# An FFT-and-experts kernel: the first batch's first stage is emptied without its scale, turned in fp32 by TensorE and split afterwards, with a new set of order constants

## The chip, the cores and the metric

The kernel runs on one core of one Trainium2 chip. The metric is the device time of one execution in microseconds (us); the medians are over three executions. TensorE is called PE here, VectorE DVE, ScalarE ACT, GpSimd POOL and SyncE SP, as the profile does.

## What is computed

Two parts follow each other. The first is a frequency-domain mixing layer, the second a top-1 mixture of experts on its output:

```python
X = np.fft.rfft(x, axis=1)                 # x: 8 batches x 2496 x 256
Yr = Xr @ w_r - Xi @ w_i + b_r
Yi = Xr @ w_i + Xi @ w_r + b_i
Y = soft_threshold(Yr, 0.01) + 1j * soft_threshold(Yi, 0.01)
y = np.fft.irfft(Y, n=2496, axis=1)        # 19968 tokens x 256

logits = y @ w_gate                        # 8 experts
e = argmax(logits); gate = softmax(logits)[e]
eom = sigmoid(y @ w_output_gate)[e]
out = gate * eom * (relu(y @ w1[e]) @ w2[e])   # 256 -> 1024 -> 256
```

## The kernel before

The transform of length 2496 = 39 x 64 is done in two stages of matrix products. For each of the 8 batches:

- **Stage 1** (`stage1_pair`, 11 pairs a batch): x as fp32 is the stationary operand, the 39-point table `f1t` the moving one. The result of a pair fills a PSUM bank. ACT and DVE empty it into the tile `at`, as a high and a low half in fp16 (L730, L731). Both are multiplied by the batch's scale `sx`, a power of two that `scales` works out from the squares and maxima of the whole batch (L444, L591, L628 to L630, a maximum over partitions through PE at L479, then L461 to L466).
- **The turn** (`load_a`): `at` has to be transposed, 10 pieces `p` of two planes each, into the ring of tiles `A`. Pieces named in `PT` are turned by PE, four fp16 products with the identity for each plane (L764), and emptied by ACT or DVE (L768, L769); the others by a transposing DMA of SP's queue (L750).
- **Stage 2** (L799, table `ct`), emptied into `xt` by ACT, DVE and one negation (L810, L811, L813 or L814); **the mixing** (L823 with the bias, L829 with the weights `whl`, 25 products for each of 10 steps), soft threshold into `z` and `zhl` (L844 to L849); **stage 3** (L859, table `gt`) into `bt`; a transposing DMA into `bdt` (L899); **stage 4** (L925), written to DRAM as `yd`.
- The gate's logits (L970, L980), and each token's rank in its expert. When four batches are through, and again when all eight are, the `routing` passes build lists of tokens by products of one-hot tiles (`ol`, `ob`; L1361, L1362, L1383, L1391 on PE). `indices` and `factors` end a pass (L1235, L1236).

The experts' part works on 160 tiles of 128 tokens. The tokens of a tile are gathered by an indirect DMA of POOL (L1491), scaled and split by DVE and ACT (L444, L1543, L1544), and transposed by DMA into `eT`. For two tiles of one expert, `up` makes four banks of 12 products each (L1651), emptied into `hh` by ACT (L1661) and then DVE (L1662). `down` makes 24 products for each tile in two halves of 12 (L1612). The first half reads what came from the first two banks of `up`, the second what came from the other two. A tile's result goes through ACT (L1628) and an indirect DMA of POOL (L1631) to the output. 18 tiles are shared by two experts ("mixed", with weights in `latebt` and `latebdt`).

While x of the first batch lands, `warm` puts products of a constant tile (L605) on PE wherever the plan has a gap before its time `WARM`.

The order of all this is not written out. Every operation asks for an engine with a due time, and the class `Issue` plays the engines forward with a duration for each operation: a free engine takes the ready operation with the earliest due time. The result is a fixed order of instructions for each engine; on the chip an engine works through its list and waits at semaphores. Due times are built from some sixty constants (`P`, `TP`, `TE`, `SA`, `UP`, `DN` and so on), so a change of them changes the order and nothing else. A name `bs` or `b` below is the mixing bias, `mx` the scale's partial sums, `yms` and `ymd` a tile's maxima.

Of the kernel before, what the change touches and what calls it, by code (L numbers as in the profile page):

```python
# [14 lines left out]
F32 = mybir.dt.float32  # L15
# [118 lines left out]
ET = mybir.EngineType  # L134
ORDERED = {ET.PE, ET.Activation, ET.DVE, ET.Pool, ET.SP}

P = 69.09
TP, TE, QT = -17.42, -31.89, 23.82
PT = (0, 1, 2, 3, 6, 8), (0, 1, 3, 6)
DK = 2.8  # L140
T1 = 0.91
S2 = 21.69
E1 = 55.44
DS = 3.78
ES = 11.46
Z1 = 52.83
Z2 = 35.62
IV = 0.04
IS = 2.69
GO = -30.77  # L150
R0 = 32.01
R1, G1 = -16.38, 0.17
GA = 0.7
W0 = 5.47
W1 = 30.1
TG = 33.24
HEAD = 15.0
LAG = dict(P=0.17, A=0.16, D=0.14, G=0.09, S=0.0)

RATE = 225e3  # L160
TAIL = 1.7
XL, TA, TB, YS, WL, WS = -73.83, -22.34, -36.29, 66.21, 6.06, 105.43

EARLY = dict(yg=3, yhl=2, eT=1, hh=1, o=1)
PLACES = dict(yg=6, yhl=5, eT=3, hh=2, o=5)
UP, DN = 1.08, 10.48
AHEAD = 6
FLUSH = {*range(T_A, T_ALL - 20, 16), *range(T_ALL - 20, T_ALL - 8, 4)}
# [3 lines left out]
LR = 10.75
QN, QY, QV, QX, QZ, QU = -2.96, 6.37, 247.7, 109.12, 39.86, 94.12
RA, QE = -34.21, -24.82
SA = 23.55
SE = 86.03
Z3 = -31.18
BE = 53.36
YE = 61.11
PB = -5.56, 0.44, 0.72, 8.7, 1.32, -0.16, 7.74, 6.51  # L180
XC = 7.0, 0.1, 5.4, 0.1, 3.0, 0.1
GL = 0.6
RT = -58.7
WT = 0.0
WF = -7.7
QO = -74.27
CB = 4
WARM = 40.0
OL = 2, 3
# [144 lines left out]
def tile_fft_moe(ctx, tc, x, w_r, w_i, b_r, b_i, w_gate, w_og, w1, w2, f1, f4, cmat, gmat, m16, out, dbg=None):  # L334
# [375 lines left out]
    def stage1_pair(b, g, r):  # L710
        xs = xt[b, g // 2]
        j0 = 2 * (g % 2)

        def f(i):
            pt = bank(i)
            pv = pt[:, :480].rearrange("p (k c w) -> p c k w", c=2, w=12)
            for j in range(2):
                for dh in range(2):
                    k, m = (P3, 6) if g < 10 else (2 * N1, 4)
                    fw = f1t[:k].rearrange("p (k c) -> p k c", c=6)[:, :, :m]  # L720
                    T.matmul(pv[:, dh, :, m * j:m * j + m], xs[:k, j0 + j, 128 * dh:128 * dh + 128], fw, start=True, stop=True)  # L721
            return pt[:, :480].rearrange("p (k c w) -> p k c w", c=2, w=12)

        i, pv = yield "P", r, T1, f, True
        used(b, g // 2)
        yield "sx", b
        sx = st[b, "sx"]
        m = 12 if g < 10 else 8
        hi, lo = (at[:, :, :, v, 12 * g:12 * g + m] for v in range(2))
        yield "A", r - SA, 0.66, lambda: A.activation(hi, pv[:, :, :, :m], AF.Copy, scale=sx)  # L730
        yield "D", r - SA, 0.68, lambda: V.scalar_tensor_tensor(lo, pv[:, :, :, :m], sx, hi, ALU.mult, ALU.subtract)  # L731
        io.free(i)
        give("s1")
        st[b, "n1"] += 1
        if st[b, "n1"] == 11:
            io.set("s1", b)

    def load_a(b, r):

        yield "s1", b  # L740
        if b == 0:
            yield "whl"
        for p in range(NP):
            yield slots["A"]
            a = st[b, "A", p] = ring(pm, [128, KP, 2, 2, 128], F16, "A", AN)
# [12 lines left out]

# [58 lines left out]
    def mix(b, p, r, xt_):  # L817
# [906 lines left out]
```

## Time and profile before

| | us |
|---|---|
| median of 3 executions (1417.12 to 1421.66) | 1419.6 |
| the profiled execution | 1415.86 |
| its span, first to last instruction | 1414.0 |
| PE busy | 1388.8 |
| DVE busy | 958.4 |
| ACT busy | 733.4 |
| POOL busy | 641.9 |

The span is what the trace covers; 1.9 us lie around it. A matmul's busy time is its latency, and neighbours overlap: 24 products of 256 columns that follow each other take 2.62 us in the chain of waits, 0.109 us each, though each shows 0.27 us of busy time. So a busy PE says that there was always a product under way, and the work itself is counted by the distance from one product to the next.

### The profile page before, as it was taken

Reading aid. Unit: us, or ns where it says so; the run is one execution under the profiler, and the core shown is the slowest. Engines: PE = TensorE matmul, PEld = TensorE weight load, DVE = VectorE, ACT = ScalarE, POOL = GpSimd, SP = SyncE. Lnnn points to the kernel's source line nnn. Section 1 sums busy time; section 2 is a strip of 40 time slices with the busy share of each in tenths; the row PEclk is TensorE's granted clock in tenths of the full one; section 3 lists DMA queues with packets and bytes.
Section 4 is the critical chain, followed back from the end, with each engine's and each line's share of the span. In section 5 each row is a group of like instructions: output and inputs, shape, how many; then the busy total and the mean of one; then the engine's idle time right before and its main releaser. Section 6 shows DMA issues by size and latency. Waiting matters only on the chain.

```text
span 1414.0 us, 40457 instructions
## 1 busy us (share of the span) xinstructions
PE 1388.8 (98%) x15696; PEld 1234.6 (87%) x15696; DVE 958.4 (68%) x2591; ACT 733.4 (52%) x1389; POOL 641.9 (45%) x718
## 2 busy tenths in 40 slices
PE   7999999999999999999999999999999999999998
PEld 5998888888888888888888888899999899899997
DVE  5787888789999887688899855454454455445441
ACT  4877777778786855444333344343343334334342
POOL 3464654446567655235554443334433433433322
PEclk9999999999999999999999999999999999999999
DMA  8699999998989696889562274556643566457541
GB/s 202 175 182 232 206 220 209 238 195 225 227 206 224 172 210 164 211 177 233 160 165 69 68 195 83 132 124 147 139 120 83 142 159 160 114 136 156 138 116 34
DMA packets 285994, 231.51 MB, mean 164 GB/s; under 512 B 239246, under 2 KB 248080, under 8 KB 279167
## 3 DMA queue, kind: packets, MB, share of 16 engines
q1 hardware_dynamic: 270377, 187.02, 56.0%
q0 software_dynamic: 15424, 41.90, 13.0%
q8 instruction: 123, 2.02, 0.6%
q14 instruction: 70, 0.57, 0.1%
HBM read 286.72 MB, written 58.52 MB: 244 GB/s over the span
## 4 chain that ended last, share of the span: by engine, by line
PE 80%; DVE 7%; issue 4%; DMA 3%; POOL 3%; SPq 1%; ACT 1%; POOLq 0%; ACTq 0%; DVEq 0%
PE ps L1651 26%; PE ps L1612 26%; PE ps L829 11%; PE ps L721 4%; PE ps L925 3%; PE ps L799 3%; PE ps L859 3%; POOL out L1631 1%; DMA x<-in_x 1%; PE ps L970 1%; DMA bdt<-bt 1%; PE ps L823 1%; PE ps L764 1%; PE ps L605 1%; DVE bt L875 1%
## 5 line engine op out<-in xcount | busy, mean ns | idle before, releaser
L1612 PE MATMUL ps<-wbuf,hh 128*128 128x256 f16 x3408 | 389.8, 273 | 0.0
L1651 PE MATMUL ps<-eT,wbuf 128*128 128x256 f16 x3408 | 387.5, 273 | 0.0
L1662 DVE SCALAR_TENSOR_TENSOR hh<-ps,hh 128x512 f16<-128x512 f32 x284 | 196.0, 691 | 254.3 <-ACT hh L1661 253.5
L1612 PEld LDWEIGHTS <-hh 128*128 128x128 f16 x3408 | 328.9, 98 | 42.0 <-issue 3.8
L1651 PEld LDWEIGHTS <-wbuf 128*128 128x128 f16 x3408 | 330.1, 98 | 40.2
L1631 POOL DMA_INDIRECT out<-o,sidx x160 | 165.2, 1033 | 361.7 <-ACT o L1628 334.7
L1661 ACT ACTIVATE hh<-ps 128x512 f16<-128x512 f32 x284 | 169.5, 597 | 237.0 <-PE ps L1651 235.1
L1491 POOL DMA_INDIRECT yg<-yd,gidx x160 | 163.1, 1020 | 137.5 <-DVE yhl L1544 81.1
L829 PE MATMUL ps<-whl,xt 128*128 128x256 f16 x1920 | 222.6, 273 | 0.0
L829 PEld LDWEIGHTS <-xt 128*128 128x128 f16 x1920 | 187.5, 98 | 31.6 <-issue 1.2
L1628 ACT ACTIVATE o<-ps,facd 128x256 f32<-128x256 f32 x142 | 67.0, 472 | 141.5 <-PE ps L1612 100.8
L1543 ACT ACTIVATE yhl<-yg,yss 128x256 f16<-128x256 f32 x142 | 68.2, 502 | 69.1 <-DVE yssi L455 53.6
L721 PE MATMUL ps<-f1t,x 117*128 117x120 f32 (+1 forms) x704 | 88.5, 280 | 8.3 <-DMA x<-in_x 8.0
L721 PEld LDWEIGHTS ps<-f1t,x 117*128 117x128 f32 (+1 forms) x704 | 84.6, 195 | 11.6 <-issue 9.6
L849 POOL TENSOR_TENSOR zhl<-z,zhl 128x512 f16<-128x512 f32 x63 | 75.3, 1196 | 28.4 <-ACT zhl L847 25.3
L848 POOL CAST zhl<-z 128x512 f16<-128x512 f32 x47 | 30.1, 641 | 109.5 <-DVE z L845 78.1
L1544 DVE SCALAR_TENSOR_TENSOR yhl<-yg,yss,yhl 128x256 f16<-128x256 f32 x142 | 66.8, 487 | 8.8 <-ACT yhl L1543 6.9
L844 ACT ACTIVATE zhl<-ps,sc 128x512 f32<-128x512 f32 x80 | 54.7, 686 | 32.6 <-PE ps L829 28.4
L1662 DVE SCALAR_TENSOR_TENSOR lategt<-ps,lategt 128x512 f16<-128x512 f32 x36 | 24.8, 688 | 68.8 <-ACT lategt L1661 68.8
L845 DVE SCALAR_TENSOR_TENSOR z<-ps,zhl 128x512 f32<-128x512 f32 x80 | 54.7, 685 | 20.0 <-ACT zhl L844 18.5
L1128 POOL TENSOR_TENSOR wsp<-wr,wsp 128x512 f16<-128x512 f32 x54 | 66.1, 1224 | 4.5
L925 PE MATMUL ps<-bdt,f4t 120*117 120x512 f16 x264 | 67.7, 379 | 0.0
(245 smaller groups left out, 2100.5 us busy)
## 6 DMA issues: line engine op xcount, KB each, us to landing
wbuf<-wd SPq DMA_DIRECT2D x142, 1024.0 KB
latebt<-wd SPq DMA_DIRECT2D x36, 1024.0 KB
latebdt<-wd SPq DMA_DIRECT2D x36, 1024.0 KB
yd<-yt SPq DMA_DIRECT2D x120, 158.4 KB
x<-in_x SPq DMA_DIRECT2D x106, 156.0 KB
wr<-in_moe_w SPq DMA_DIRECT2D x32, 512.0 KB
wd<-wsp SPq DMA_DIRECT2D x64, 256.0 KB
yg<-yd,gidx POOLq DMA_INDIRECT x160, 3.4
```

The source lines that it names most:

```text
L721: T.matmul(pv[:, dh, :, m * j:m * j + m], xs[:k, j0 + j, 128 * dh:128 * dh + 128], fw, start=True, stop=True)
L829: T.matmul(yp[:, 256 * j:256 * j + 256], xt_[:, v, 2 * dh + j, 64 - 64 * u:192 - 64 * u], whl[:, dh, vw, 256 * u:256 * u + 256], start=Fal ...
L849: yield either("G", r - Z3, 1.2, "D", r - Z3 + QY, 1.0, lambda e: e.tensor_tensor(zhl[:, 1], z, zhl[:, 0], ALU.subtract))
L925: T.matmul(pt[:P3], w, src[:, :, :, vb_], start=(n == 0), stop=(n == 2))
L1491: yield "G", r + 5.6 * POS[t] - 30, 1.0, lambda: G.indirect_dma_start(out=yg, out_offset=None, in_=src, in_offset=bass.IndirectOffsetOnAxi ...
L1543: yield "A", r - 10, 0.5, lambda: A.activation(yhl[:, 0], yg[:, :256], AF.Copy, scale=s)
L1612: T.matmul(st["pt", t][1][c * q:c * q + c, :256], hh[:, v, fc, 128 * n + c * q:128 * n + c * q + c], wq[:, fc // 2, vw, fc % 2], start=(fc ...
L1628: yield "A", r - DN, 0.47, lambda: A.activation(o, pt[:, :256], AF.Copy, scale=fac)
L1631: yield "G", r - DN, 1.0, lambda: G.indirect_dma_start(out=outs[POS[t] % 8], out_offset=bass.IndirectOffsetOnAxis(ap=sidx[:, t:t + 1], axi ...
L1651: T.matmul(pt[:, 128 * m * j:128 * m * (j + 1)][:, 64 * q:128 * m - 64 * (len(w) - 1 - q)], wq[:, dh, g // 4, vw, 128 * (g % 4):128 * (g % ...
L1661: yield "A", r, 0.6, lambda: A.activation(hv[:, 0], pt, AF.Relu)
L1662: yield "D", r, 0.69, lambda: V.scalar_tensor_tensor(hv[:, 1], pt, 0.0, hv[:, 0], ALU.max, ALU.subtract)
```

## The change

Three things. For batch 0, stage 1 is emptied by one operation, an unscaled copy in fp32 into the same memory as `at` (seen as fp32 through `at32`). It no longer waits for `sx`. The turn of batch 0 is done by PE alone, in fp32 (`turn_0`): four transposing products for a piece `p`, all in one bank; then ACT and DVE scale and split it into `A`. For this an fp32 identity is made by POOL once, in memory of `bdt`. The wait for the mixing weights `whl` moves from the start of the turn to the mixing. Last, all the constants of the order have new values.

```diff
-P = 69.09
-TP, TE, QT = -17.42, -31.89, 23.82
+P = 69.0665505
+TP, TE, QT = -40.317835, -48.0018785, 46.5639872
...
-UP, DN = 1.08, 10.48
+UP, DN = 3.5154488, -2.4275374
...
     at = pm.tile([128, K1, 2, 2, 128], F16, name="at")
+    at32 = at.rearrange("p k c v n -> p k c (v n)").bitcast(F32)
+    eye32 = bdt.rearrange("p a n -> p (a n)")[:, :256].bitcast(F32)
+    G.tensor_copy(eye32, t16[:, M16 - 256:M16 - 128])
...
         i, pv = yield "P", r, T1, f, True
         used(b, g // 2)
+        m = 12 if g < 10 else 8
+        if b == 0:
+            raw = at32[:, :, :, 12 * g:12 * g + m]
+            yield [("A", r - SA, 0.62, lambda: A.activation(raw, pv[:, :, :, :m], AF.Copy)),
+                   ("D", r - SA, 0.68, lambda: V.tensor_copy(raw, pv[:, :, :, :m]))]
+            io.free(i)
+            give("s1")
+            st[b, "n1"] += 1
+            if st[b, "n1"] == 11:
+                io.set("s1", b)
+            return
         yield "sx", b
...
     def load_a(b, r):
 
         yield "s1", b
-        if b == 0:
-            yield "whl"
         for p in range(NP):
             yield slots["A"]
             a = st[b, "A", p] = ring(pm, [128, KP, 2, 2, 128], F16, "A", AN)
+            if b == 0:
+                io.go(turn_0(p, a, r + 2 * DK * p + TP))
+                continue
...
+    def turn_0(p, a, r):
+
+        def f(i):
+            pt = bank(i)
+            for k in range(KP):
+                for dh in range(2):
+                    m = 256 * k + 128 * dh
+                    T.transpose(pt[:, m:m + 128], at32[:, KP * p + k, dh], eye32)
+            return pt.rearrange("p (m n) -> p m n", n=128)
+
+        i, pt = yield "P", r, 0.46, f, True
+        yield "sx", 0
+        sx = st[0, "sx"]
+        hi, lo = (a.rearrange("p k c v n -> p (k c) v n")[:, :, v] for v in range(2))
+        yield "A", r - TE, 0.6, lambda: A.activation(hi, pt, AF.Copy, scale=sx)
+        yield "D", r - TE, 0.68, lambda: V.scalar_tensor_tensor(lo, pt, sx, hi, ALU.mult, ALU.subtract)
+        io.free(i)
+        st["ta", 0] = st.get(("ta", 0), 0) + KP
+        io.set("ap", 0, p)
...
         yield "sc", b
+        yield "whl"
         i, yp = yield "P", r, 2.85, f, True
```

Lines of the changed kernel stand 3 (from L501) to 35 (from about L820) further down: L594 is the old L591, L608 the old L605, L833 the old L799, L844 the old L810, L857 and L863 the old L823 and L829, L1647 and L1686 the old L1612 and L1651. New are L732 and L733 (raw copies), L778 (transposing products), L785 and L786 (high and low half). Over the whole program PE loses 28 of 52 constant products and 48 of 272 fp16 turning products and gains 40 transposing ones; SP loses 4 transposing DMAs.

How the order of ACT changes at the start, batch 0. First before; `at` is stage 1's result, `junk,mx` a square of x:

```order
L403 ACTIVATE isc<-cnt_81 128x8
L591 ACTIVATE junk,mx_144<-x 117x1024 x3
L730 ACTIVATE at<-ps_151,sx_263 128x40x12
L730 ACTIVATE at<-ps_156,sx_263 128x40x12
L730 ACTIVATE at<-ps_162,sx_263 128x40x12
L730 ACTIVATE at<-ps_168,sx_263 128x40x12
L730 ACTIVATE at<-ps_193,sx_263 128x40x12
L730 ACTIVATE at<-ps_199,sx_263 128x40x12
L730 ACTIVATE at<-ps_214,sx_263 128x40x12
```

And in the changed kernel, the same place:

```order
L403 ACTIVATE isc<-cnt_81 128x8
L594 ACTIVATE junk,mx_145<-x 117x1024
L732 ACTIVATE at<-ps_152 128x40x12
L732 ACTIVATE at<-ps_157 128x40x12
L732 ACTIVATE at<-ps_164 128x40x12
L732 ACTIVATE at<-ps_171 128x40x12
L594 ACTIVATE junk,mx_145<-x 117x1024
L732 ACTIVATE at<-ps_198 128x40x12
L732 ACTIVATE at<-ps_204 128x40x12
L594 ACTIVATE junk,mx_145<-x 117x1024
```

Before, all three squares of ACT come first and the eleven banks wait behind `sx`; in the changed kernel they are emptied between the squares, and `sx` is first read in the turn.

PE at the end of batch 0's stage 1, before (one product of each bank is shown; every one is preceded by its weight load):

```order
L721 MATMUL ps5_325<-f1t_84,x_80 128x20x4 x4
...
L605 MATMUL ps4_363<-one16_86 128x512
...
L764 MATMUL ps5_371<-t16_83,at_119 128x128
...
L764 MATMUL ps2_380<-t16_83,at_119 128x128
...
L764 MATMUL ps7_386<-t16_83,at_119 128x128
...
L764 MATMUL ps3_392<-t16_83,at_119 128x128
...
L764 MATMUL ps6_397<-t16_83,at_119 128x128
```

And in the changed kernel:

```order
L608 MATMUL ps3_292<-one16_86 128x512
L778 MATMUL ps6_302<-bdt_118,at_119 128x128 x4
L778 MATMUL ps5_309<-bdt_118,at_119 128x128 x4
L778 MATMUL ps4_314<-bdt_118,at_119 128x128 x4
L778 MATMUL ps1_325<-bdt_118,at_119 128x128 x4
L778 MATMUL ps7_331<-bdt_118,at_119 128x128 x4
L778 MATMUL ps2_337<-bdt_118,at_119 128x128 x4
L608 LDWEIGHTS one16_86
L608 MATMUL ps0_346<-one16_86 128x512
```

The first six pieces are now turned one after the other ahead of the first constant products of that stretch; before, a bank held one plane, and 12 constant products stood between the last pair and the turn.

PE in the experts' part, near the program's end, first before. One row stands for the 12 products of a bank or of a half; `hh1` is what the two `wbuf0` banks of `up` go to:

```order
L1651 MATMUL ps5_24559<-eT2_9869,wbuf0_9248 128x256
...
L1651 MATMUL ps3_24577<-eT2_9869,wbuf0_9248 128x256
...
L1651 MATMUL ps2_24592<-eT2_9869,wbuf0_9248 128x256
...
L1651 MATMUL ps0_24626<-eT2_9869,wbuf0_9248 128x256
...
L1612 MATMUL ps7_24540<-wbuf2_9512,hh0_9664 128x256
...
L1612 MATMUL ps4_24662<-wbuf2_9512,hh0_9664 128x256
...
L1612 MATMUL ps1_24691<-wbuf0_9248,hh1_9915 128x256
```

And in the changed kernel, the banks `ps2_24547` (just ahead of these rows) and `ps4_24583` being the ones that the first half of `down` on `hh1` reads:

```order
L1686 MATMUL ps4_24583<-eT2_9702,wbuf0_9254 128x256
...
L1686 MATMUL ps5_24599<-eT2_9702,wbuf0_9254 128x256
...
L1686 MATMUL ps3_24618<-eT2_9702,wbuf0_9254 128x256
...
L1647 MATMUL ps1_24633<-wbuf0_9254,hh1_9797 128x256
...
L1686 MATMUL ps0_24671<-eT0_9469,wbuf1_9255 128x256
...
L1647 MATMUL ps1_24633<-wbuf0_9254,hh1_9797 128x256
```

The half of `down` that follows its own banks stood 48 products behind the second of them here; now it stands 24 behind.

## Rows read from the trace of the kernel before

**Rows 1.** The page: PE's total, and its busy share in 40 equal slices of the span (tenths, 9 is 90% or more).

```profile
PE 1388.8 (98%) x15696; PEld 1234.6 (87%) x15696; DVE 958.4 (68%) x2591; ACT 733.4 (52%) x1389; POOL 641.9 (45%) x718
PE   7999999999999999999999999999999999999998
```

**Rows 2.** Busy time in stretches of the span: from and to (us), their length, then PE, weight loads, DVE, ACT and POOL (with counts), granted clock, DMA share, GB/s.

```profile
0.00:10.10 10.10, 1.04 (x2) 0.13 (x2) 0.24 (x3) 1.49 (x2) 4.03 (x11) 1.00 0.78 161
10.10:39.20 29.10, 27.94 (x208) 20.54 (x209) 22.35 (x52) 17.15 (x32) 8.29 (x7) 1.00 0.86 226
39.20:60.00 20.80, 20.80 (x243) 18.89 (x242) 12.93 (x50) 16.02 (x31) 7.15 (x9) 1.00 0.71 164
60.00:529.00 469.00, 463.63 (x5434) 411.48 (x5433) 401.93 (x1006) 345.95 (x655) 270.27 (x334) 1.00 0.92 210
529.00:660.00 131.00, 131.00 (x1262) 113.97 (x1260) 98.30 (x308) 62.74 (x122) 53.26 (x61) 1.00 0.82 194
660.00:800.00 140.00, 134.84 (x1314) 120.61 (x1312) 127.07 (x332) 48.83 (x96) 76.29 (x77) 1.00 0.50 131
916.00:1400.00 484.00, 484.00 (x6074) 436.81 (x6072) 230.17 (x652) 192.27 (x362) 174.81 (x174) 1.00 0.54 129
1400.00:1414.00 14.00, 9.54 (x110) 8.33 (x108) 0.00 (x0) 1.90 (x4) 4.58 (x5) 0.98 0.12 39
```

**Rows 3.** PE in order of time in the first 40 us, equal neighbours merged: start, length of the row, line, tiles, form, count, and idle time before with what ended it.

```profile
10.16 5.56 PE L721 MATMUL ps<-f1t,x 117*128 117x120 f32 x32 [8.04 <-DMA x<-in_x]
17.34 2.91 PE L721 MATMUL ps<-f1t,x 117*128 117x120 f32 x24 [0.21 <-issue]
23.29 3.83 PE L605 MATMUL ps<-one 128*128 128x512 bf16 x12 [0.38 <-DVE ma L484]
28.28 2.80 PE L721 MATMUL ps<-f1t,x 117*128 117x120 f32 x24
33.51 1.95 PE L764 MATMUL ps<-t,at 128*128 128x128 f16 x32
35.30 2.17 PE L799 MATMUL ps<-ct,A 128*128 128x128 f16 x36
37.31 1.89 PE L605 MATMUL ps<-one 128*128 128x512 bf16 x8
39.25 2.79 PE L829 MATMUL ps<-whl,xt 128*128 128x256 f16 x24
```

**Rows 4.** PE's groups in the first 39.2 us: busy time and mean ns of one, then idle time before.

```profile
L605 PE MATMUL ps<-one 128*128 128x512 bf16 x50 | 13.7, 388 | 1.9 <-DVE mx L618 1.1 <-DVE ma L484 0.4
```

**Rows 5.** DVE from 20 us on, in order of time.

```profile
21.04 0.17 DVE L628 SCALAR_TENSOR_TENSOR mx<-mx 128x6 f32<-128x6 f32 x1
23.83 0.15 DVE L466 TENSOR_SCALAR sx<-p2e 128x1 int32<-128x1 int32 x1
24.39 1.22 DVE L444 TENSOR_REDUCE mx<-x 117x1 f32<-117x1024 f32 x1
25.53 6.33 DVE L731 SCALAR_TENSOR_TENSOR at<-ps,sx,at 128x480 f16<-128x480 f32 x10
34.16 3.08 DVE L769 CAST A<-ps 128x512 f16<-128x512 f32 x5 [1.20 <-PE ps L764]
37.23 1.87 DVE L811 SCALAR_TENSOR_TENSOR xt<-ps,xt 128x512 f16<-128x512 f32 x3
```

**Rows 6.** ACT and POOL in the same stretch.

```profile
20.25 1.06 ACT L591 ACTIVATE junk<-x 117x1024 bf16<-117x1024 f32 x1 [1.69 <-DMA x<-in_x]
24.08 4.62 ACT L730 ACTIVATE at<-ps,sx 128x480 f16<-128x480 f32 x8 [2.68 <-DVE sx L466]
38.00 1.77 ACT L814 ACTIVATE xt<-xt 128x512 f16<-128x512 f16 x3
23.33 2.13 POOL L561 TENSOR_TENSOR whl<-wr,whl 128x1024 f16<-128x1024 f32 x1
```

**Rows 7.** The negation of `xt` where DVE makes it (L813): ns shortest/middle/longest.

```profile
L813 DVE TENSOR_SCALAR xt<-xt x29: 278/294/1230, 81.4 to 514.0; 128x512 f16<-128x512 f16 x29
```

**Rows 8.** A piece of the chain of waits: start, length, and the count of stage 1's products that follow each other.

```profile
239.27 9.84 PE ps L721 x88
```

**Rows 9.** Who PE waited for in the whole run: us in total, times, longest.

```profile
PE ps L1391 <- POOL ob L1383: 5.2, 7, 1.3
PE ps L980 <- DVE lb L974: 1.7, 1, 1.7
PE ps L859 <- POOL zhl L849: 1.2, 2, 1.0
PE ps L859 <- POOL zhl L848: 0.8, 1, 0.8
```

**Rows 10.** A block of the experts' part in order of time: `up` from 906.88, its banks through ACT and DVE, then `down`.

```profile
906.88 5.40 PE L1651 MATMUL ps<-eT,wbuf 128*128 128x256 f16 x48
910.38 0.69 DVE L1662 SCALAR_TENSOR_TENSOR hh<-ps,hh 128x512 f16<-128x512 f32 x1 [0.62 <-ACT hh L1661]
912.12 2.13 PE L1612 MATMUL ps<-wbuf,hh 128*128 128x256 f16 x18
912.30 0.73 DVE L444 TENSOR_REDUCE ymd<-yg 128x1 f32<-128x256 f32 x2
```

**Rows 11.** Indirect gathers and their wait around the second routing pass, 800 to 900 us: who waited for whom.

```profile
POOL yg L1491 <- DVE yhl L1544: 35.9, 7, 5.6
```

More of the change, by code (lines that the diff above doesn't have):

```diff
@@ L135 @@
 ORDERED = {ET.PE, ET.Activation, ET.DVE, ET.Pool, ET.SP}
-P = 69.09
-TP, TE, QT = -17.42, -31.89, 23.82
+P = 69.0665505
+TP, TE, QT = -40.317835, -48.0018785, 46.5639872
 PT = (0, 1, 2, 3, 6, 8), (0, 1, 3, 6)
-DK = 2.8
+DK = 2.9023332
 T1 = 0.91
[L142 to L156, printed above, removed]
+S2 = 20.2569054
+E1 = 57.9258585
+DS = 4.08956
+ES = 9.177749
+Z1 = 90.093383
+Z2 = 36.1627438
+IV = 2.0067704
+IS = 3.2556534
+GO = 5.0416869
+R0 = 46.6676556
+R1, G1 = -27.5455943, 0.1
+GA = 0.5808308
+W0 = 7.200579
+W1 = 30.1170607
+TG = -21.6966264
 HEAD = 15.0
@@ L161 @@
 TAIL = 1.7
-XL, TA, TB, YS, WL, WS = -73.83, -22.34, -36.29, 66.21, 6.06, 105.43
+XL, TA, TB, YS, WL, WS = -76.6365295, -40.537833, -97.8030735, 69.0876097, 31.2711338, 100.7997022
 EARLY = dict(yg=3, yhl=2, eT=1, hh=1, o=1)
 PLACES = dict(yg=6, yhl=5, eT=3, hh=2, o=5)
-UP, DN = 1.08, 10.48
+UP, DN = 3.5154488, -2.4275374
 AHEAD = 6
@@ L171 @@
 S1 = 6
[L172 to L180, printed above, removed]
+LR = -9.092333
+QN, QY, QV, QX, QZ, QU = 45.6175552, 96.5836618, 166.2823519, 55.7725734, 4.9558306, 101.1480836
+RA, QE = -78.0167507, -189.4826202
+SA = 26.9991574
+SE = 100.9865002
+Z3 = -61.6084018
+BE = 85.6474188
+YE = 28.9068519
+PB = -6.9899331, -1.6940119, 0.2169427, 8.9834992, 1.4717145, 3.3327762, 6.8599759, 8.2019982
 XC = 7.0, 0.1, 5.4, 0.1, 3.0, 0.1
 GL = 0.6
-RT = -58.7
+RT = -96.6439604
 WT = 0.0
-WF = -7.7
-QO = -74.27
+WF = 12.7803097
+QO = -61.4159383
 CB = 4
@@ L725, in stage1_pair @@
         used(b, g // 2)
+        m = 12 if g < 10 else 8
[9 more added lines that the diff above has]
+            return
         yield "sx", b
         sx = st[b, "sx"]
-        m = 12 if g < 10 else 8
         hi, lo = (at[:, :, :, v, 12 * g:12 * g + m] for v in range(2))
@@ L751, in load_a @@
             io.at(io.now + TAIL, io.set, "ap", b, p)
-        while st.get(("ta", b), 0) < KP * len(PT[b > 0]):
+        while st.get(("ta", b), 0) < KP * (len(PT[1]) if b else NP):
             yield 0.5
```

## The prediction

> **What bounds the kernel now.** I read the page first. PE is busy 98% of the span, and in 40 slices only the first and the last are visibly short of it [rows 1]. So no other engine bounds the kernel as a whole, and the next view is busy time by stretch [rows 2]: the reader is to see where PE's column falls short of the length. It does in the first 10.1 us (x is on its way), a little up to 39.2, by 5.4 us between 60 and 529, by 5.2 between 660 and 800, and by 4.5 behind the last product. From 39.2 to 60, from 529 to 660 and from 916 to 1400 nothing is missing.
>
> Busy is not useful, though. Up to 39.2 us PE makes 50 products of a constant tile (L605), 13.7 us of busy time [rows 4] and some 10.8 us of issue time at 0.215 us each (the row of 8 at 37.31, 1.89 us less the last one's 0.39, over seven steps [rows 3]). They fill waits. What PE has to do up to the first mixing at 39.25 [rows 3] is small: 88 records of stage 1 at 0.112 us (9.84 us for 88 [rows 8]), 9.9 us; 32 turning products at 0.056 (1.95 us less a latency of 0.22, over 31 steps [rows 3]), 1.8; 36 products of stage 2 at the same distance, 2.0; three small maxima, 0.2. That is 13.9 of 39.25 us, so 25.4 us of the start are wait or filler. After it the lists are full: no filler between 39.2 and 60 and no idle time [rows 2].
>
> So the start is worth what brings the first mixing forward, and a microsecond won there reaches the end if no later stage takes it back.
>
> **The change part by part.**
>
> *Why the first mixing is late.* x's last part lands at 20.25 (ACT's square starts then [rows 6]), and `sx` is made at 23.83 [rows 5]. Only then do the eleven banks empty: ten low halves on DVE take 6.33 us, 0.63 each [rows 5]. ACT's eight high halves start with `sx`, at 24.08 [rows 6]. The last pairs of stage 1 stand behind for want of a bank (28.28 [rows 3]), then come the turn at 33.51, stage 2 at 35.30 [rows 3], its evictions and negations (ACT, from 38.00 [rows 6]), mixing at 39.25.
>
> *What is taken out of that.* The raw copies run between the squares, while x lands. PE's remaining pairs need no freed bank: after x's last part at 20.25, four pairs at 0.9 us from 17.34 are done at about 20.9, two more by 22.7, the maximum, and the eleventh by 23.9. ACT copies it by about 24.6. Ahead of `sx` on DVE stands one raw copy more (0.62, as the copies L769 [rows 5]), in front of the sum at 21.04 [rows 5]; half of it fits into a wait for ACT's square that follows, so `sx` comes 0.2 to 0.5 later, say at 24.2.
>
> *The new chain.* PE makes four constant products (to 24.8), then 24 transposing ones for six pieces. The trace has none of these. Bounds: 0.056 us as the fp16 turn, and 0.224 as an fp32 product, which the trace shows as two records (a batch has eleven pairs of four in the code, and 88 records [rows 8]). I take 0.112, one such record, as the data are fp32 and one pass needs one weight load of that type. The turn ends at 27.5, six constant products at 28.8. DVE is slower: after `sx` five or six small operations on scale factors (to 25.2), a maximum of batch 1's x (1.22 [rows 5]) to 26.4, six low halves at 0.63 to 30.2, two low halves of stage 2 at 0.62 (1.87 for three [rows 5]) to 31.5, one or two negations at 0.29 [rows 7] and the semaphores: the first mixing starts at 32.1. ACT's high halves run just ahead of it. `whl`, whose wait is now here, was done at 25.5 on POOL (23.33 + 2.13 [rows 6]); the fp32 identity, a short copy on POOL, lies in the idle time before it and costs nothing. The first half of `ct` has landed when the old run has its second half on the way; stage 2 asks for it at 28.8.
>
> So the mixing starts 39.25 - 32.1 = 7.15 us earlier. What PE still owes then differs by the turn: before 16 fp16 products (0.9 us), now four transposing ones (0.45). **Start: -7.6 us.** With 0.056 a product the mixing still waits for DVE, and it is -7.8. With 0.224 the turn ends at 30.2, stage 2 starts at 31.5 behind the six fillers, the mixing at 34.8, and the rest costs 0.9: -4.5.
>
> The Trainium skill states, in "TensorE: Matmul & The Clock Gate", Terms, that trn2's transpose mode is four times faster for FP32. By it a product costs the lower bound, and the sum would be -7.8. No row here has one.
>
> *Does PE stay fed from 32.1 on?* In the changed order two mixings follow each other (2.85 us each), then 24 products of stage 2, a turn, the third mixing. DVE needs per step a low half of the turn, one of stage 2, the negation and the threshold, about 0.63 + 0.62 + 0.29 + 0.7, that is 2.2 us, against 4.2 or more of PE. I count no new wait.
>
> *Wait removed at SP.* Four transposing DMAs of batch 0 leave the queue. Nothing on PE waited for them (no such row among PE's waits [rows 9]): nothing.
>
> *The new constants.* They move everything between 60 and 916 us, but not the number of products. What they can win is bounded by PE's idle time there, 5.4 + 5.2 = 10.6 us [rows 2]. What they can lose the old trace can't show. I looked at how far a consumer stands behind its producer, in PE's own work. Between a mixing and its stage 3, seven of 80 were closer than 4.6 us before and four are now. Between the gate's products and L980, which cost 1.7 us in one place [rows 9], four of eight were closer than 1 us and none is now. That speaks for a small gain. Against it: in the stage with the 5.2 us, where PE waits for POOL's `ob` [rows 9] while DVE is busy 127 of 140 us [rows 2], POOL gets 49 of these multiplications instead of 44, and the stage moves later. I take zero, with both ends, -10 and +10, kept.
>
> Behind 916 us, PE loses nothing but the tail, and the tail is the same: last `down`, ACT, the scatter.
>
> **Sum.** 1415.86 of the profiled execution - 7.6 = 1408.3. The median of the three runs lies 3.7 above that execution, so 1419.6 - 7.6 = **1412.0**.
>
> **The rivals.**
>
> *The gain is taken back at the second routing pass (no change).* The experts' 65th tile needs its end. In the old order 719 products (78 us) lie between the last row of `factors` on DVE and the `up` of that tile; in the new one 167, that is 18 us. Between them a maximum (0.73 for a pair [rows 10]), scale, split, a transposing DMA: by these rows some 10 to 14 us. The old gathers were so far ahead that they waited 35.9 us for a free place [rows 11]; that reserve is gone. If DVE, 91% busy there, comes more than 5 us late, PE waits for the rest. A lateness of 10 costs 5, one of 15 costs 10: 1417 to 1422. Chance 0.18.
>
> *Slower: `down` now follows its `up` too closely.* A half of `down` stands 24 products (2.62 us) behind its second bank in 75 of 302 places, before in 19. The chain needs, by the old block: second bank ended at 906.88 + 24 x 0.109 = 909.50, DVE done at 910.38 + 0.69 = 911.07, so 1.6 us [rows 10]. There is 1.0 us to spare. It decides once DVE has more than 1.0 us of other work in front: a pair's maxima are 0.73 [rows 10], and with the scale's small operations it is over 1.5. If that fell into half of the 56 new places at 0.7 us each, the loss would be 20 us: 1419.6 - 7.6 + 20 = 1432. Against it: two evictions lie between, and the order doesn't put the groups together. Chance 0.10.
>
> *TensorE's clock falls in the turn.* In the old trace PE begins at the lower of its two levels: the first 32 records take 5.56 us, where at the later distance of 0.112 they would take 3.75 (31 steps and one latency of 0.28); the 24 at 17.34 take 2.91, which is that later distance [rows 3]. From there on the 50 fillers leave PE no long idle time. The new order has 28 fillers fewer and a turn of 2.7 us. If the clock fell and came back as at the start, it would cost what it cost there, 5.56 - 3.75 = 1.8 us, twice that if the mixing itself is hit: 1414 to 1416. The Trainium skill says, in the same page, Part 4: PE-mode transpose, that transposing products don't bring the full clock; by that rule, the trace would show 1.2 GHz behind the turn. But fillers and stage 2 stand directly behind. Chance 0.07.
>
> *The middle gets shorter as well.* Half of the 10.6 us goes: 1407. Chance 0.2.
>
> **How the numbers follow.** My forecast, the start alone with a middle within 3 us of the old, has 0.45. Less than 0.3% (4.3 us) can't be told from no change. Faster, below 1415.3: forecast 0.42 of its 0.45, the shorter middle 0.2, most of the clock's case 0.05, a little of the first rival: 0.69. Slower, above 1423.9: the close `down` 0.10, and 0.02 of the routing pass: 0.12. Between them 0.19. The range takes the shorter middle at its end (1412 - 10) and the first rival nearly whole: 1402 to 1421. It leaves out the slower rival.
>
> **What would show each step.** First mixing (L863) at 31 to 33 us, and no idle PE up to 60. `sx` at about 24.2. Distances of L778 of 0.05, 0.11 or 0.22 tell its price. Idle of PE between 60 and 529 near 5, near 5 in the routing stage, none from 916 on; idle before L1647 with DVE `hh` as its releaser would be the slower rival, and before L1686 around the 65th tile the first one. A mixing before 33 us with a time above 1416 would mean that the order lost in the middle what the start won, and that I was wrong to take it as neutral.

## The result: the start came as forecast, and the experts' part lost twice as much

| | before | changed |
|---|---|---|
| median, us | 1417.04 (1415.2 to 1421.66, 8 runs) | 1427.26 (1422.43 to 1437.45, 8 runs) |
| ratio, 95% interval | | 1.0074 (1.0048 to 1.01): 0.7% slower |
| the profiled execution, us | 1415.86 | 1426.43 |
| its span, us | 1414.0 | 1424.6 |

The forecast was 1412.0, with a range of 1402 to 1421. Direction and range were both wrong.

The view to start with is the one of [rows 2], busy time by stretch, now of the changed kernel (us; then PE, PEld, DVE, ACT, POOL busy; PEclk, DMA share, GB/s):

```profile
10.10:39.20 29.10, 29.10 (x249) 26.07 (x250) 20.73 (x51) 21.42 (x38) 9.80 (x9) 1.00 0.93 242
39.20:60.00 20.80, 20.80 (x235) 19.60 (x233) 18.18 (x58) 15.39 (x31) 7.73 (x10) 1.00 0.53 152
60.00:529.00 469.00, 461.83 (x5410) 408.17 (x5408) 404.90 (x980) 345.19 (x663) 275.66 (x340) 1.00 0.89 208
529.00:660.00 131.00, 129.76 (x1238) 113.28 (x1237) 71.20 (x209) 58.32 (x115) 48.92 (x56) 1.00 0.74 176
660.00:800.00 140.00, 138.33 (x1310) 122.37 (x1309) 127.15 (x372) 54.71 (x105) 71.00 (x76) 1.00 0.55 146
800.00:916.00 116.00, 113.39 (x1071) 101.45 (x1069) 88.12 (x247) 44.21 (x86) 52.09 (x53) 1.00 0.53 128
916.00:1400.00 484.00, 473.74 (x5888) 426.25 (x5886) 225.89 (x650) 186.97 (x355) 169.68 (x172) 1.00 0.53 129
```

The reader is to see the last line. From 916 to 1400 us PE was idle for nothing before [rows 2] and is idle for 10.3 us now. Between 60 and 529 it lacks 7.2 us (5.4 before), between 529 and 916 together 5.5 (5.2 before). What ends the idle time behind 916 us, in the view of waits (us in total, times, longest):

```profile
PE ps L1686 <- DMA eT<-yhl: 5.3, 3, 2.2
PE ps L1686 <- issue: 5.0, 2, 2.8
```

L1686 is `up`. It waits for the transposing DMA of the tokens. There are five such waits, before the products at 941.6, 1024.4, 1118.7, 1200.8 and 1346.6 us; measured by the distance between neighbours less the usual 0.109, they are 1.2, 3.0, 2.3, 2.2 and 2.4 us, 11.1 together. The view names a DMA for three and nothing for two; all five have the same place, the first bank of a pair, 8.2 to 9.9 us after SP issued that pair's second transposing DMA. The second one had a sequel (PE's timeline; start, duration of the row, shape, count, idle before):

```profile
1020.14 1.47 PE L1647 MATMUL ps<-wbuf,hh 128*128 128x256 f16 x12
1024.41 1.89 PE L1686 MATMUL ps<-eT,wbuf 128*128 128x256 f16 x12 [2.80 <-issue]
1026.10 2.76 PE L1647 MATMUL ps<-wbuf,hh 128*128 128x256 f16 x12
1028.66 1.51 PE L1686 MATMUL ps<-eT,wbuf 128*128 128x256 f16 x12
```

Twelve products of `down` take 2.56 us from their start to the next row, 0.213 each. That is the lower of the clock's two levels (1.2 of 2.4 GHz), and the granted clock of the stretch, the last number but two, is 0.66:

```profile
1024.00:1029.00 5.00, 4.59 (x27) 3.52 (x28) 1.08 (x2) 1.05 (x3) 0.57 (x1) 0.66 0.62 248
```

It costs 1.6 us more. 11.1 + 1.6 = 12.7 us behind 916 us, where the old trace has none of it. Summed over the trace, distances longer than usual cost 14.4 us more than before. The 28 missing fillers give 6.0 us back, and the turn's products take 1.7 more (40 at 0.109 for 48 at 0.056). That makes +10.1 of the +10.6 us between the two profiled executions.

### The profile page after: what moved, and what is told of

Its sections match the earlier page's. It is cut to its first block, busy times and chain, and to the rows that moved or that the text cites. A ratio compares the mean times of both kernels' runs of the same rounds, so it can differ in the third digit from the quotient of the medians.

```text
span 1424.6 us, 40459 instructions
## 1 busy us (share of the span) xinstructions
PE 1388.2 (97%) x15660; PEld 1235.5 (87%) x15660; DVE 960.9 (67%) x2570; ACT 733.9 (52%) x1400; POOL 643.8 (45%) x731
## 4 chain that ended last, share of the span: by engine, by line
PE 75%; DVE 11%; DMA 5%; issue 5%; POOL 1%; SPq 1%; ACT 1%; POOLq 0%; ACTq 0%; DVEq 0%
PE ps L1647 24%; PE ps L1686 23%; PE ps L863 10%; PE ps L724 5%; PE ps L960 3%; PE ps L833 3%; PE ps L894 3%; DMA eT<-yhl 2%; DMA bdt<-bt 1%; DVE ol L1396 1%; DVE hh L1697 1%; DMA x<-in_x 1%; PE ps L857 1%; DVE ob L1397 1%; POOL out L1666 1%
## 5 line engine op out<-in xcount | busy, mean ns | idle before, releaser
L1686 PE MATMUL ps<-eT,wbuf 128*128 128x256 f16 x3408 | 404.7, 273 | 10.7 <-DMA eT<-yhl 5.7
L1647 PE MATMUL ps<-wbuf,hh 128*128 128x256 f16 x3408 | 405.2, 273 | 0.8 <-DVE hh L1697 0.7
L1686 PEld LDWEIGHTS <-wbuf 128*128 128x128 f16 x3408 | 330.1, 98 | 54.7 <-issue 15.1
L1647 PEld LDWEIGHTS <-hh 128*128 128x128 f16 x3408 | 331.0, 98 | 41.9 <-DVE hh L1697 1.2
L1526 POOL DMA_INDIRECT yg<-yd,gidx x160 | 158.1, 988 | 228.4 <-DVE yhl L1579 197.5
L863 PE MATMUL ps<-whl,xt 128*128 128x256 f16 x1920 | 222.6, 273 | 0.0
L863 PEld LDWEIGHTS <-xt 128*128 128x128 f16 x1920 | 187.8, 98 | 32.1 <-issue 1.3
L884 POOL TENSOR_TENSOR zhl<-z,zhl 128x512 f16<-128x512 f32 x70 | 82.2, 1175 | 38.5 <-ACT zhl L882 33.9
L724 PEld LDWEIGHTS ps<-f1t,x 117*128 117x128 f32 (+1 forms) x704 | 84.7, 197 | 11.3 <-issue 8.7
L833 PE MATMUL ps<-ct,A 128*128 128x128 f16 x960 | 65.0, 219 | 0.2 <-DVE ste L912 0.2
L894 PE MATMUL ps<-gt,zhl 128*128 128x128 f16 x960 | 64.8, 219 | 0.2 <-POOL zhl L884 0.2
```

Source lines behind the costliest of these rows:

```text
L833: T.matmul(pt[:, 128 * (2 * dh + j):128 * (2 * dh + j) + 128], a[:, (k1 + j) % KP, dh, v], ct[:, k1 + j, vc], start=(n == 0), stop=(n == 2))
L863: T.matmul(yp[:, 256 * j:256 * j + 256], xt_[:, v, 2 * dh + j, 64 - 64 * u:192 - 64 * u], whl[:, dh, vw, 256 * u:256 * u + 256], start=Fal ...
L884: yield either("G", r - Z3, 1.2, "D", r - Z3 + QY, 1.0, lambda e: e.tensor_tensor(zhl[:, 1], z, zhl[:, 0], ALU.subtract))
L894: T.matmul(bv[:, j], zhl[:, vz, c:c + 128], gt[:, 2 * p + j, v], start=(n == 0), stop=(n == 2))
L1526: yield "G", r + 5.6 * POS[t] - 30, 1.0, lambda: G.indirect_dma_start(out=yg, out_offset=None, in_=src, in_offset=bass.IndirectOffsetOnAxi ...
L1647: T.matmul(st["pt", t][1][c * q:c * q + c, :256], hh[:, v, fc, 128 * n + c * q:128 * n + c * q + c], wq[:, fc // 2, vw, fc % 2], start=(fc ...
```

## Why the DMA is late: the four banks of an `up` are spread out

Before, an `up` of two tiles was one piece of 48 products, and the `down` of another pair behind it likewise (PE's timeline of the kernel before):

```profile
985.39 5.40 PE L1651 MATMUL ps<-eT,wbuf 128*128 128x256 f16 x48
990.63 5.40 PE L1612 MATMUL ps<-wbuf,hh 128*128 128x256 f16 x48
```

In the changed kernel banks of `up` and halves of `down` alternate:

```profile
994.84 1.47 PE L1686 MATMUL ps<-eT,wbuf 128*128 128x256 f16 x12
996.15 1.47 PE L1647 MATMUL ps<-wbuf,hh 128*128 128x256 f16 x12
997.46 1.47 PE L1686 MATMUL ps<-eT,wbuf 128*128 128x256 f16 x12
998.77 1.47 PE L1647 MATMUL ps<-wbuf,hh 128*128 128x256 f16 x12
1000.08 1.47 PE L1686 MATMUL ps<-eT,wbuf 128*128 128x256 f16 x12
1001.39 2.78 PE L1647 MATMUL ps<-wbuf,hh 128*128 128x256 f16 x24
1004.01 1.47 PE L1686 MATMUL ps<-eT,wbuf 128*128 128x256 f16 x12
```

First to last product: 5.1 us before; now 10.4 for about half of the pairs, as here, and 6.5 for the others. There are three places of eT for pairs, and `tokens` goes on with the pair three further on only when the last bank is done. So that pair's preparation begins 5.3 us later, while its own `up` does not move. I call **lead** the time from SP's issue of a pair's second transposing DMA to the pair's first `up` product. SP's rows, of the changed kernel for the pairs of 1024.41 and 1052.68, then of the kernel before for the one of 1023.87:

```profile
1014.50 1.69 SPq L1592 DMA_TRANSPOSE eT<-yhl  x1
...
1045.46 1.20 SPq L1592 DMA_TRANSPOSE eT<-yhl  x1
```

```profile
1011.00 1.46 SPq L1557 DMA_TRANSPOSE eT<-yhl  x1
```

1052.68 - 1045.46 = 7.2 us, without a wait; 1024.41 - 1014.50 = 9.9, of which PE waited 3.0; before, 1023.87 - 1011.00 = 12.9. Over the 36 pairs behind 930 us the shortest lead fell from 12.5 to 6.9; 14 pairs are ordered with about 7 (PE's wait taken off), and PE waited at five of them. What distinguishes the five is what SP issued just ahead of that DMA: a piece of new weights for a shared tile (`wd` into `latebt` or `latebdt`, 1 MB). SP's row of such an issue is 0.35 or 0.36 us long where the piece moves, and 0.07 or 0.08 where the expert is still the same and nothing moves. Ahead of the DMAs of 1014.50 and of 1045.46:

```profile
1013.67 0.36 SPq L1502 DMA_DIRECT2D latebt<-wd  x1
...
1044.91 0.08 SPq L1502 DMA_DIRECT2D latebt<-wd  x1
```

Six of the 14 have a piece 0.4 to 0.8 us ahead; five of them waited, and one (`up` at 1291.05) did not. Four others have a piece of `wbuf` 2.9 to 3.7 us behind the DMA, four have none within that time, and none of these eight waited. Before, the same six pairs had a piece 0.8 to 1.6 us ahead as well, and with leads of 12.9 us or more none waited. In these traces a wait came only where both met, the piece and the short lead. The DMA share, the last number but one, is 0.95 to 1.16 around the five, 0.90 around the sixth and 0.33 to 0.81 around the eight; two stretches with a wait and one without:

```profile
1014.00:1024.00 10.00, 7.62 (x70) 6.58 (x68) 4.70 (x13) 3.61 (x7) 2.40 (x3) 1.00 1.16 175
1045.00:1053.00 8.00, 8.00 (x75) 7.17 (x74) 3.43 (x7) 3.34 (x6) 2.19 (x3) 1.00 0.50 93
1109.00:1119.00 10.00, 7.82 (x73) 6.79 (x71) 4.73 (x13) 3.54 (x7) 2.48 (x3) 1.00 1.02 169
```

So the theory tested, **L**: UP and DN, which place the banks of `up` and the halves of `down`, cut the lead, and where an expert's new weights come in, PE waits.

## The experiments

One thing first. The first fifteen runs fell on three chips on which the kernel before takes 1452 to 1459 us, 36 to 42 more than in the result; the last three on one where it takes 1416.7, as in the result. So a time is compared only with that of the kernel before on the same chip. A run's own trace is comparable with others of its kind of chip.

**One half of the change alone** (e1 and, on another chip, e6; e15 once more on the chip of e12; e2).

```diff
 e1, e6, e15: the changed code
-P = 69.0665505        (and all the other new constants)
+P = 69.09             (all the old ones)
 e2: the code before, with all the new constants
```

> The new code with all constants of the kernel before. Theory L (the loss is made by UP and DN alone: the four banks of an `up` are spread over 10.4 us instead of 5.1, so a place of eT comes free 5.3 us later and the next transposing DMA has 6.0 us instead of 11.3 until its `up`): no such spread here, so no wait before `up` from 916 us on, and the start's gain of 6 to 7 us reaches the end: 1417 - 6.5 = about 1410.5 (1408 to 1413). Rival G (whatever is won at the start is lost again on the way, by what follows the turn, whatever the constants): about 1417. First mixing near 33 us in both.

> The old code with all the new constants. Theory L: the five waits before `up` between 941 and 1347 us are there again, 12 to 13 us together, and the first mixing stands near 39 us as before: 1417 + 10 to 17, about 1430 (1426 to 1435). Rival G (the new turn makes the loss): near 1417, at most 1420.

> The new code with all constants of the kernel before, a second time. Where the kernel before takes about 1417: theory L (UP and DN make the loss) 1408 to 1413; rival G (what the start wins is lost on the way) about 1417, and G': the old constants fitted to the old code lose more in the middle, as in the first run of it, 1420 to 1424. No wait before `up` for eT in any of them.

> The new code with the old constants once more, without the shortening, beside the others of this call. Theory M (the old constants, fitted to the old code, lose the start's gain between 60 and 530 us, 5.7 us at the first mixing and -3 at the first `up`): 5 to 10 above the kernel before; first mixing near 34 us, first `up` near 538 against 535.

Measured: e1 1459.5 against 1452.8, ratio 1.0047 (1.003 to 1.0064); e6 1462.3, 1.0052 (1.0028 to 1.0076); e15 1463.0, 1.0039 (1.002 to 1.0058); e2 1461.6, 1.0057 (1.0037 to 1.0078). Neither half is faster. For the code alone my theory L had said that the start's gain reaches the end, and that is false: the first mixing of e6 is at 34.1 us, against 39.7 in a trace of the kernel before on such a chip (e11), but its first `up` at 538.0 against 535.1. The old constants lose 8.5 us between (the kernel before stands at 537.0 in e12, whose list is the same up to there, so the size is rough), for instance in these waits from 60 to 529 us of e6, none of which the old trace has in this size [rows 9]:

```profile
PE ps L960 <- ACT yt L964: 2.8, 1, 2.8
PE ps L960 <- DVE ste L912: 1.9, 1, 1.9
PE ps L857 <- DVE ste L912: 1.7, 1, 1.7
```

Work that begins 6 us earlier meets other neighbours. M, of e15, holds for the places (first mixing 33.8, first `up` 539.3) and nearly for the size, 4.0 us instead of 5 to 10.

**UP and DN, and WF** (e3 and, on another chip, e7; e8 the other way round; e4).

```diff
 e3, e7: the changed kernel          e8: the kernel before, the other way
-UP, DN = 3.5154488, -2.4275374
+UP, DN = 1.08, 10.48
 e4: the changed kernel
-WF = 12.7803097
+WF = -7.7
```

> The changed kernel with UP and DN alone put back to 1.08 and 10.48. Theory L: an `up` of two tiles takes 5.1 us again, PE has no idle time in 916 to 1400 us, 12.7 us come back: 1427.3 - 12.7 = about 1414.5 (1411 to 1418). Rival S (what counts is SP's queue: the weights' fetches, moved by WF, stand in front of the second transposing DMA of a pair and hold it 4.3 us): the waits stay, 1424 to 1430.

> The changed kernel with UP and DN alone put back, a second time. Where the kernel before takes about 1417: theory L 1411 to 1418, no wait before `up` for eT behind 916 us. Rival S (SP's queue, not the spread of `up`): waits of 8 us or more remain, 1424 to 1430. Rival R: the waits go, but the routing passes lose as much (waits for `ob` over 10 us in 660 to 860), 1422 to 1430.

> The kernel before with UP and DN alone set to the new 3.515 and -2.428. Where the kernel before takes about 1417: theory L: an `up` is spread over 6.4 or 10.4 us and waits for eT appear behind 916 us where weights of the next expert are fetched, 8 to 13 us, 1425 to 1430. Rivals S and R: no or hardly any such wait, 1415 to 1420.

> The changed kernel with WF alone put back from 12.78 to -7.7, which gives the weights' fetches other places in SP's queue. Rival S: the second transposing DMA of a pair is no longer held, the five waits go: 1414 to 1418. Theory L: an `up` is still spread over 10.4 us, the waits stay at about 8 to 15 us: 1424 to 1430.

| | shortest lead behind 930 us | time, ratio to before |
|---|---|---|
| kernel before (e11) | 11.2 | 1454.0 |
| e1, code alone | 11.4 | 1.0047 |
| e7, UP and DN put back | 12.2 | 1468.6, 1.0094 (1.0066 to 1.0123) |
| changed kernel (e5) | 7.0 | 1455.9, 1.0023 (0.9997 to 1.0048) |
| e2, new constants alone | 7.0 | 1.0057 |
| e4, WF put back | 7.0 | 1454.1, 1.0006 (0.9993 to 1.0019) |
| e8, UP and DN alone | 7.0 | 1461.2, 1.0053 (1.0032 to 1.0074) |

The lead follows UP and DN in both directions, whatever the other constants are, and not WF. With WF put back, waits for eT of 3.7 us stay in e4, so rival S is out; e4's time, that of the kernel before, does not decide it, as the changed kernel itself is only 0.2 to 0.3% off on such chips (e5, and e10 below). The time does not follow as L had it. L wanted 12 to 13 us of waits for eT behind 916 us in e2, 8 to 13 in e8 and 8 to 15 in e4; there are 0.2, 0.2 and 3.7. e8 did lose 8.7 us, but its large wait stands elsewhere, at 619.93 us, where SP's queue has three transposing DMAs of `bdt` (14.0 us) ahead of that pair's (waits of e8 from 529 to 916 us):

```profile
PE ps L1651 <- DMA eT<-yhl: 6.3, 1, 6.3
```

e3 took 1470.5, ratio 1.0126 (1.0107 to 1.0145), although no wait for eT is left in it behind 916 us. Rival R, written down for e7, explains part. The waits for `ob` in the routing stretch, 529 to 916 us, of e7 and of the changed kernel (e5):

```profile
PE ps L1426 <- POOL ob L1418: 12.3, 11, 3.3
```

```profile
PE ps L1426 <- POOL ob L1418: 4.2, 4, 1.8
```

So the same two constants also set how routing products lie between `up` and `down`. And the waits for eT, which L needs, are small on these chips, whichever the order: 0.3 us behind 916 in e5.

**Put back only behind the routing** (e9, with the changed kernel e10 and the kernel before e11 on the same chip).

```diff
-UP, DN = 3.5154488, -2.4275374
+UP, DN = (lambda t: 1.08 if POS[t] >= 72 else 3.5154488), (lambda t: 10.48 if POS[t] >= 72 else -2.4275374)
```

> The changed kernel with UP and DN put back for tiles from the 73rd on alone; TensorE's list is that of the changed kernel up to a point behind the last routing product, so the routing passes keep their order. Theory L: an `up` takes 5.1 us from there on, each transposing DMA has 11 us or more until its `up`, and the waits for eT behind 916 us go. Where the kernel before takes about 1417: 1427 - 12 = 1415 (1412 to 1418). On a chip like that of the runs so far (kernel before 1452.5, changed kernel 1456, waits for eT of about 2 us): 1453 to 1457. Rival S (SP's queue): as the changed kernel in both cases, and the waits stay.

> The changed kernel itself on the chip of this call. Where the kernel before takes about 1417: 1427, waits for eT of 11 to 13 us. Where it takes 1452: 1452 to 1458, waits for eT of 1 to 4 us.

> The kernel before itself, for a trace of it on the chip of this call. Where it takes about 1417: PE idle for 10 to 11 us between 60 and 800 and not at all from 916 to 1400. Where it takes 1452: gaps that nothing releases, 35 to 41 us together as in the other runs there, mostly behind 916 us in the products of the shared tiles; the waits that something releases are the 10 us of the trace of before.

e9 took 1463.9, ratio 1.0063 (1.004 to 1.0086); e10 1456.9, 1.0029 (1.0007 to 1.0051); e11 1454.0. Waits behind 916 us, first of e10, then of e9, then of e11:

```profile
PE ps L1647 <- issue: 17.6, 34, 1.1
PE ps L1686 <- DMA eT<-yhl: 3.2, 2, 2.6
```

```profile
PE ps L1686 <- issue: 14.1, 33, 1.2
PE ps L1647 <- issue: 6.8, 11, 1.0
```

```profile
PE ps L1651 <- issue: 10.6, 25, 1.2
```

The waits for eT go, and e9 is still 7 us slower than e10. In the profiled executions (1465.5 and 1454.8) the loss does not lie behind the routing. PE's lists of e9 and e10 are the same up to the first bank of the 37th pair, and there e9 is already 11.3 us behind (first e10, then e9):

```profile
947.64 1.47 PE L1686 MATMUL ps<-eT,wbuf 128*128 128x256 f16 x12
...
958.95 2.78 PE L1686 MATMUL ps<-eT,wbuf 128*128 128x256 f16 x24
```

From there to the end of the span e9 takes 504.8 us and e10 505.4. What fills both behind 916 us are waits that nothing releases, 20.9 us in e9 and 18.2 in e10. Where they lie is seen in e10's timeline, in the products of a tile that two experts share:

```profile
1022.51 0.27 PE L1647 MATMUL ps<-latebdt,lategt 128*64 128x256 f16 x1 [0.20 <-issue]
...
1023.27 0.27 PE L1647 MATMUL ps<-latebt,lategt 128*64 128x256 f16 x1 [0.27 <-issue]
1023.98 0.29 PE L1647 MATMUL ps<-latebdt,lategt 128*64 128x256 f16 x1 [0.44 <-issue]
```

After its 96 products of 64 columns, 0.029 us apart, and among the 48 of half width that follow, two for each 0.109 us, single products stand 0.5 to 0.7 us apart. The same stretch in the trace of the result has no such gap.

**The gaps taken away** (e12 to e14). In all three, a shared tile takes one expert's weights for all of its tokens and leaves the other's out, with the other engines' lists unchanged:

```diff
-                for q, wq in enumerate(w):
+                for q, wq in enumerate(w[:1]):
...
-                            tok = eT[:, :m, v, dh] if len(w) == 1 else eT[:, 0, v, dh, 64 * q:64 * q + 64]
+                            tok = eT[:, :m, v, dh]
```

> The kernel before, but a shared tile takes the first expert's weights for all of its 128 tokens: 48 products of 128 columns instead of 96 of 64, and 24 of full width instead of 48 of half width for `down`. That computes something else for half of these tokens; PE's time for the products stays about the same, with half the instructions. Theory I (the gaps that nothing releases come from PE's instructions running dry in those dense products): gaps behind 916 us from 26 to under 6 us, time 1453 - 22 = 1428 to 1434. If the gaps have another cause they stay and so does the time, 1450 or more.

> The changed kernel with the same shortening of the shared tiles. Theory I takes its gaps (32 us behind 916 us) to under 6. Theory L (the lead of 6 us is too short where an expert's new weights are fetched) then brings the waits for eT back, 7 to 13 us behind 916 us: 1455 - 28 + 8 = about 1435 (1432 to 1440), 2 to 8 above e12. Without L the waits stay under 4 us: 1424 to 1429.

> The changed kernel with UP and DN put back for tiles from the 73rd on, and the same shortening. Theory L: lead 11 us, no wait for eT behind 916 us, 6 to 12 us faster than e13: 1424 to 1431. Rival (the spread of `up` is the better order in itself, as the 7 us between the third chip's two runs of it would say): 3 to 8 us slower than e13.

The kernel before took 1459.0 on this chip; e12 1431.7, e13 1429.9, e14 1431.0. The time came as theory I had it: with half the instructions for the shared tiles' products 27 us are gone, of which some 4 are PE time (18 tiles, 0.24 us less each by the distances). These products also became twice as wide, so e12 does not tell the number of instructions from their width. The waits for eT came back in e13, at the six pairs with a piece of weights just ahead, the one that did not wait in the result among them, but smaller than L's 7 to 13; e14 has one left, ahead of 1000 us, and gaps elsewhere (both behind 916 us):

```profile
PE ps L1686 <- DMA eT<-yhl: 3.9, 4, 2.2
PE ps L1686 <- issue: 1.3, 2, 0.6
PE ps L1647 <- issue: 0.8, 2, 0.4
```

```profile
PE ps L1686 <- issue: 4.7, 10, 1.0
PE ps L1686 <- DMA eT<-yhl: 2.6, 1, 2.6
```

In time the two can't be told apart, against L's 6 to 12 us.

**Every transposing DMA twice** (e16 to e18: e12 to e14 with the line below). The added one writes memory that nothing reads.

```diff
-        yield from move(r - 10, 1.4e5, 1.2, lambda: nc.sync.dma_start(eT..., yhl..., transpose=True))
+        yield from move(r - 10, 1.4e5, 1.2, lambda: [nc.sync.dma_start(a..., yhl..., transpose=True) for a in ([parts_["dup"][:, POS[t] % 6]] if "dup" in parts_ else []) + [eT]])
```

> The kernel of e12 with each transposing DMA of eT preceded by a second one of the same data into memory that nothing reads, from about 620 us on; the other engines' lists are those of e12. A transposing DMA takes SP 1.2 us to issue, so the second tile of a pair lands 2.5 us or more later. Theory L: lead 11 us, so hardly any new wait: e12 + 0 to 4, about 1433. Without L (the DMA itself or SP's queue is the limit): as much loss as in e17.

> The kernel of e13 with the same doubling. Theory L: half of the 36 pairs behind 930 us have a lead of 6 us, of which the five late landings already used up all; 2.5 us less gives waits for eT of 1 to 4 us in 12 to 18 places, 15 to 45 us together: e13 + 15 to 45, 1445 to 1475. Without L: e13 + 0 to 5.

> The kernel of e14 (UP and DN put back from the 73rd tile on) with the same doubling. Theory L: e14 + 0 to 6, at most 1437, and 10 us or more faster than e17, as the lead is 11 us behind 930 us. Without L: as much above e14 as e17 is above e13.

Now on a chip like that of the result (kernel before 1416.7): e16 1410.0 (1409.1 to 1412.8), e17 1435.3 (1433.3 to 1439.8), e18 1424.7 (1413.3 to 1428.8). The list of e18 is that of e17 up to the 37th pair, and its leads are long again from 1000 us on. Waits from 1000 us on, first e16, then e17, then e18:

```profile
PE ps L1653 <- DMA lategt<-yhl: 0.2, 1, 0.2
```

```profile
PE ps L1688 <- issue: 5.9, 3, 3.2
PE ps L1688 <- DMA eT<-yhl: 4.0, 2, 2.7
```

```profile
PE ps L1688 <- DMA lategt<-yhl: 0.6, 2, 0.5
```

9.9 us against 0.6. From the first bank of the 37th pair, the last place that the lists of PE share (950.1 us in e17, 957.1 in e18), e17 takes 482.3 us to the end and e18 468.8, so 13.5 less. The medians differ by 10.7; the profiled executions by only 6.5, as that of e18 is a long one (its ten runs go from 1413.3 us at a granted clock of 0.998 to 1428.8 at 0.994). With these two changes made, on this kind of chip, the lead made by UP and DN behind the routing decides, and the order before, with its lead of 9 us and more even so, has nothing to wait for.

The waits of e17 behind 916 us stand at 950, 1033, 1126, 1208, 1300 and 1356 us, at the same six pairs as in e13, and at no other short lead. 15 to 45 us in 12 to 18 places were expected of it; it came to 13.9 in six. Behind three of them PE ran at the lower level, as here from 948 us on, and so from 1126 to 1130 and from 1300 to 1304 (0.57 each), which costs 6.1 us more by the distances of the products:

```profile
948.00:956.00 8.00, 5.90 (x30) 4.17 (x31) 1.08 (x2) 1.46 (x3) 0.98 (x1) 0.57 0.38 73
```

The other 14.6 of the 25 us between e17 and e16 are between e18 and e16. In the profiled executions e18 has 16.9 us more idle PE than e16 ahead of 1000 us. 10.7 lie between 529 and 1000, where e18 still has the new order with its short leads and waits 11.0 us for eT. The other 6.2 lie between 60 and 529, where no lead plays a part.

## Why the prediction was wrong, by its own steps

**The start: right.** Predicted: first mixing at 32.1 us; it stands at 32.87, against 39.25 [rows 3]. The transposing product was taken at 0.112 us, between bounds of 0.056 and 0.224:

```profile
24.55 2.78 PE L778 MATMUL ps<-bdt,at 128*128 128x128 f32 x24
...
32.87 2.78 PE L863 MATMUL ps<-whl,xt 128*128 128x256 f16 x24
```

From 24.55 to the next row at 27.17 it is 2.62 us, 0.109 each. The Trainium skill's rule in "TensorE: Matmul & The Clock Gate", Terms, by which the cost is the lower bound, does not hold here. The granted clock stayed at 1.00 through the turn (10.1 to 39.2 above), so the clock's rival did not show: fillers and stage 2 lay around it. The Trainium skill's rule in the same page, Part 4: PE-mode transpose, by which transposing products don't bring the full clock, did not show either.

**The middle: within its ends, but not neutral.** The gain of 6.4 us at the first mixing is 3.0 at the first `up` (532.0 before, 529.05 now). Zero with ends of 10 covered that. These are one trace each, and eleven traces with the changed kernel's list up to there place the first `up` between 527.4 and 536.5 us, so the 3.4 us lost are not clear of that scatter. The runs e1, e6 and e15 show that even the old constants would have lost the start's gain there, on their chips.

**The routing rival: did not come.** The routing columns ended at 850.9 us instead of 795.5, and the 65th tile's `up` had nothing to wait for; the idle time of 529 to 916 is the old one within 0.4 us.

**The slower rival: right in its stage, wrong in its mechanism.** It said that `down` would follow its `up` too closely; PE waited 0.7 us for `hh` in the whole trace. The same spreading did the harm at the other end, in how long it holds eT.

**The step that failed** is "Behind 916 us, PE loses nothing but the tail". I had the shuffled `up` and `down` before me and looked only at the distance from `up` to its own `down`, a product for which PE waits. I did not look at what the last bank releases: the place of eT, and with it the next pair's maxima, scale, split and transposing DMA. That term was put at zero and was 12.7 us: 11.1 of waits and 1.6 of lower clock. The forecast also started 2.6 us too high, from 1419.6, the median of three runs; that of all eight is 1417.0. From there the measured terms give 1417.0 - 6.4 at the first mixing + 3.4 from there to the first `up` + 12.7 = 1426.7, near the 1427.3 measured. By the prediction's last sign, a mixing before 33 us and a time above 1416, the loss would lie in the middle; 3.4 us of it do, and 12.7 do not.

**What stays open.** On the chip of the result the changed kernel was not run with UP and DN put back alone; that it would come near 1415 there is worked out, not shown. e16 to e18 show what the lead does there only with the shared tiles shortened and the DMAs doubled. Why e9 is late ahead of the first product that it orders anew, no run tells. Why some chips show the gaps and others don't, no run tells. No version that computes the whole and beats the kernel before was found.

## What to carry to other kernels

When an order interleaves two groups that used to be whole, look at both ends of each group: its consumers, and the buffer that its last member frees. Compute for each buffer the lead of its next writer, and compare it not with the usual landing time but with that behind the largest transfer that stands just ahead in the same queue. Constants fitted to one order are part of it: with the old ones the start's gain was gone by the first `up` (e1, e6, e15), and of new ones each has to be read for what else it moves. And before a difference between two runs is put down to a change, look where their lists part: in e9 it was there before.

## What the runs showed that was not expected

The kernel before takes 1417 us in the result and on the chip of e16 to e18, and 1452 to 1459 on three others. On the latter, dense short products (0.029 us, each with a weight load) are followed by single products 0.5 to 0.7 us apart; half the instructions there took 27 us away. And one wait of 3.0 us was followed by 16 products at the lower clock level, while four waits of 1.2 to 2.4 us were not. In e17 waits of 3.9, 3.3 and 2.7 us were followed by it, and those of 1.0 to 1.7 were not. In e10 such a stretch, at 1268 us with a granted clock of 0.66 over 5 us, has no single gap over 1.11 us just ahead of it. And a wait of 3.3 us at 785.8 in e11 was followed by none.
